# A decoder block's forward and backward on one core: the two layer norms and their gradients at the turn written as sums over shared means, with weights, dV groups and d(o) reordered

## The chip, the cores and the metric

One core of a Trainium2 chip runs the whole program. The metric is device time in microseconds (us), lower is better; the kernel before was timed in three runs. Engines: TensorE (PE, with its weight loads PEld), VectorE (DVE), ScalarE (ACT), GpSimd (POOL, here mostly a queue that issues stores) and SyncE (SP, the queue that issues loads).

## The reference: what is computed

One token goes forward through an adaptive-layer-norm block, attention over a cached K and V (32 heads, 8192 positions, 192 wide) and an MLP; then the gradients of the output with respect to x, K, V, wq, wo, w3, w4, c and w_mod are taken. Cut to what matters here:

```python
def _layernorm(x, axis=-1, eps=1e-05):
    m = jnp.mean(x, axis=axis, keepdims=True)
    v = jnp.var(x, axis=axis, keepdims=True)
    return (x - m) / jnp.sqrt(v + eps)
# _A_ref: q = x @ wq per head; p = softmax(q K^T * 192**-0.5); o = p V; returns o @ wo
# _B_ref, for one token (its mixer's shifted rows are all zero, so x1 = x):
    return x + _gelu(_layernorm(x) @ w3) @ w4
# the block:
mod = (_silu(c) @ w_mod)                      # sa, ca, ga, sb, cb, gb, 640 each
h = _layernorm(x) * (1 + ca) + sa
x = x + ga * _A_ref(h, k_cache, v_cache, wq, wo)     # x1 in the kernel
h = _layernorm(x) * (1 + cb) + sb                    # h_b in the kernel
x = x + gb * _B_ref(h, w1, w2, w3, w4)
# vjp with grad_out: outputs: x, and the gradients of the nine inputs named above; dK and dV are the largest
```

So between the last head's attention and the first gradient there are two layer norms one behind the other (of x1, then of h_b), the product with w3, a gelu, the products with w4 forward and backward, w3 backward, and the two layer norms' gradients. The gradient of the attention output, d(o) = (ga * dx1) @ wo^T, is what all dK and dV need.

## The kernel before

K and V of a head are 3 MB each and are streamed in halves of 1536 KB. Position p*64 + j of the cache lies on partition p, so a half is a tile of 128 x 32 x 192. There are five buffers for K (`KB`) and three for V (`VB`).

*Forward*, `for i in range(H1)`: per head the scores are a product on VectorE (`dot_mul`, L302), a halving add (L306) and a sum on TensorE against an identity (`dot_tree`, L312). One head later the softmax weights scale V (`scale_v`: some rows on VectorE, L352, the others one by one on ScalarE, L359), and TensorE multiplies the scaled V by K (`m_units`, L374 and L379: a 193-wide product that the gradient of q needs, in four quarters). `pair_ao` multiplies the outputs of two heads by wo. `wst` holds weights in flight: one buffer for tag `w`, two for tag `wo`.

*The turn* is everything from `x, y, z = X[H1], ...` (L568) to the first pass of the backward loop. Its order on PE, DVE, ACT and SP is as written (`manual_schedule(engines=ORDER)`): each engine and each queue runs its instructions in the order in which the code names them, and one that waits holds all behind it. In the turn the last head's (31) scores are taken in quarters into `pb`, head 30's scaled V tiles `vs0` to `vs3` are made and multiplied into `mp`, head 31's output goes through `o_rows` (L394), `pair_sums`, `pair_ao` to `aoN` (L709), and:

- `g_layernorm` (L141), twice: `x1` to `n1`, `h_b` to `n2`. Each takes a mean by a matmul with a matrix of 1/640 (`mean_mm`, L123) and a sum on VectorE (L128), centres, squares, takes a second mean, and the root as exp(-0.5 ln(.)) on ScalarE (L151, L152).
- `ups` (L767): 60 matmuls with w3; then the gelu (L773 to L792). `dg_part` (L476) is the dot of one w4 row group with `dbo_bc`, 12 in all on VectorE; `du_bf` (L795) needs them all.
- `w3t_gen` (L749, L750) transposes w3 in 12 groups of 5 blocks, ScalarE copying 640 columns each; `dn_ps` (L850) is the product with it.
- `layernorm_bwd` (L166), twice, then `dao_bf` (L918), `do_mm(TL, 1)` (L901): d(o) of head 31. Head 30 follows in the first round of the loop.
- `dw4_dve` (L802): outer products for dw4, in pieces where VectorE has room.
- w3 and w4 are loaded in nine transfers, two of them during head 29, into `w4b`, `wp`, a `wo` buffer, a `vs` buffer and K buffers that came free.

*Backward*, `for s in range(NS)`, 64 half heads from head 31 down: `mul_q` (L929) multiplies V by d(o), `tree_q` (L948) sums to dP (L316), dS follows (L1244), `dk_part` (L964) makes dK, `dv_groups` (L959, L960) makes dV in eight groups by TensorE and ScalarE copies; `dk_store` (L1214) and `dv_store` (L1210) are issued by POOL. A V half is loaded four half heads ahead, when the product that read the buffer is done. `c_ps` (L1223) sums dao * AO over columns for all heads: five fp32 matmuls with 32 columns. `side` jobs (dwq, dwo, dw_mod, dw3) are spread over the slots of the rounds.

## Time and profile before

| what | us |
|---|---|
| three runs | 1414.3, 1417.39, 1418.7 (median 1417.39) |
| the profiled execution's own time | 1418.06 |
| its span | 1416.1 |
| the turn by windows: DMA share at 531 to 549 | 0.98 |
| at 549 to 561 | 0.58 |
| at 561 to 573 | 0.26 |
| at 573 to 582 | 0.12 |
| at 582 to 600 | 0.74 |
| granted TensorE clock in the same five windows | 1.00, 0.86, 0.93, 0.50, 0.78 |

Busy shares of the span: TensorE 84%, VectorE 78%, ScalarE 63%. A busy share is an average over three stages with different limits (forward, turn, backward); the shares by window tell them apart. A timeline line reads: start in us, time of the merged group, engine, line of the code, operation, output tile <- input tiles, shapes, count, and in brackets the idle time in front of it and what ended it.

### The profile page before, as it was taken

The page shows a single profiled execution, that of the slowest core. Times are in us where ns is not written, and L with a number is a line of the kernel's source. Part 1 is how long each engine was busy: PE and PEld are TensorE (multiplying, and loading weights), DVE is VectorE, ACT ScalarE, POOL GpSimd, SP SyncE. Part 2 cuts the span into 40 slices and gives each one's busy share as a digit, 9 for nine tenths or more (in the row PEclk, how much of TensorE's full clock was granted, in tenths as well). Part 3 has the DMA queues.
Part 4 walks back from the last instruction along what each step waited for, and adds up shares of the span by engine and source line. Part 5 has one row for each costly group of instructions (what it writes and reads, how often), then busy time and mean ns, then how long its engine had stood idle before and what let it go on. Part 6 is the DMA issues. An engine that isn't in the chain of part 4 may idle for free.

```text
span 1416.1 us, 30395 instructions
## 1 busy us (share of the span) xinstructions
PE 1190.1 (84%) x12697; PEld 748.8 (53%) x12697; DVE 1108.4 (78%) x1418; ACT 893.9 (63%) x1952; POOL 105.3 (7%) x190
## 2 busy tenths in 40 slices
PE   3888989999999999798867997887978787779975
PEld 2777777777777777543323443443434333334431
DVE  4989999999999997886755875676766767768775
ACT  0767777777777776465645665565655565556664
POOL 0000000000000000110100110111110101111110
PEclk9999999999999999755555555565555655555555
DMA  9999999999999997599999999999999999999998
GB/s 375 394 394 416 418 415 418 411 415 414 422 415 419 411 412 274 178 391 428 424 393 420 427 423 424 420 422 422 425 420 421 411 414 410 405 400 392 424 411 355
DMA packets 76247, 569.35 MB, mean 402 GB/s; under 512 B 7342, under 2 KB 25086, under 8 KB 36046
## 3 DMA queue, kind: packets, MB, share of 16 engines
q1 hardware_dynamic: 51210, 342.02, 59.5%
q0 software_dynamic: 24368, 224.87, 38.1%
q8 instruction: 99, 1.62, 0.4%
q10 hardware_dynamic: 532, 0.53, 0.1%
q14 instruction: 38, 0.31, 0.1%
HBM read 340.95 MB, written 226.43 MB: 401 GB/s over the span
## 4 chain that ended last, share of the span: by engine, by line
issue 47%; DVE 22%; DMA 13%; PE 10%; POOL 6%; ACT 1%; SPq 0%; POOLq 0%; DVEq 0%
DVE prod L302 9%; DMA KB<-in_A_k_cache_dram 8%; DVE prod L306 5%; DVE vs L352 3%; PE mp L374 3%; DMA out_dram<-KB 3%; POOL out_dram L1214 2%; POOL out_dram L1210 2%; DMA w_st<-in_A_wq_dram 2%; PE half_ps L312 2%; PE mp L379 2%; DMA KB<-in_A_v_cache_dram 1%; DVE pq L929 1%; POOL out_dram L1054 1%; DVE KB L964 1%
## 5 line engine op out<-in xcount | busy, mean ns | idle before, releaser
L960 ACT CAST KB<-dv_ps 128x768 bf16<-128x768 f32 x512 | 397.4, 803 | 159.7 <-PE dv_ps L959 157.6
L948 PE MATMUL dot_ps<-pq,ident_bf 128*128 128x256 bf16 x1506 | 383.6, 398 | 24.0 <-DVE dP L316 22.0
L964 DVE TENSOR_TENSOR KB<-qs_bc,dS 128x3072 bf16<-128x3072 bf16 x122 | 210.7, 1753 | 129.0 <-DMA out_dram<-KB 117.0
L359 ACT ACTIVATE vs<-VB,Ef 128x192 bf16<-128x192 bf16 x840 | 303.5, 447 | 0.0
L948 PEld LDWEIGHTS <-ident_bf 128*128 128x128 bf16 x1506 | 151.9, 124 | 179.7 <-issue 140.3
L959 PE MATMUL dv_ps<-do_r,er_b 1*128 1x192 bf16 x2048 | 231.2, 338 | 4.5 <-ACT KB L960 3.2
L929 DVE TENSOR_TENSOR pq<-VB,do_r 128x3072 bf16<-128x3072 bf16 x126 | 220.4, 1749 | 15.7 <-PE dot_ps L948 15.7
L302 DVE TENSOR_TENSOR prod<-KB,qs_bc 128x6144 bf16<-128x6144 bf16 x62 | 207.9, 3353 | 26.6 <-DMA KB<-in_A_k_cache_dram 20.3
L374 PE MATMUL mp<-vs,KB 128*128 128x193 bf16 x1968 | 189.9, 249 | 3.7 <-ACT vs L359 2.6
L374 PEld LDWEIGHTS <-KB 128*128 128x128 bf16 x1984 | 171.1, 98 | 13.1 <-DMA KB<-in_A_k_cache_dram 5.3
L822 ACT COPY wT<-wT_ps 128x1024 bf16<-128x1024 bf16 x82 | 79.0, 964 | 122.6 <-PE wT_ps L821 122.2
L959 PEld LDWEIGHTS <-er_b 1*128 1x128 bf16 x2048 | 69.4, 104 | 157.5 <-issue 154.7
L312 PE MATMUL half_ps<-prod,ident_bf 128*128 128x256 bf16 x744 | 95.1, 279 | 44.4 <-DVE prod L306 44.1
L352 DVE TENSOR_TENSOR vs<-VB,E 128x1728 bf16<-128x1728 bf16 x120 | 123.7, 1052 | 0.3 <-ACT vs L359 0.3
L306 DVE TENSOR_TENSOR prod<-prod 128x3072 bf16<-128x3072 bf16 x62 | 108.7, 1754 | 1.0
L312 PEld LDWEIGHTS <-ident_bf 128*128 128x128 bf16 x744 | 72.9, 100 | 62.7 <-issue 53.6
L379 PE MATMUL mp<-vs,KB 128*64 128x193 bf16 x1968 | 105.9, 250 | 0.0
L316 DVE TENSOR_REDUCE dP<-dot_ps 128x32 f32<-128x512 f32 x64 | 44.0, 688 | 66.9 <-PE dot_ps L948 66.6
L379 PEld LDWEIGHTS <-KB 128*64 128x64 bf16 x1984 | 79.4, 109 | 20.0 <-issue 19.9
L339 ACT ACTIVATE E<-S_h,negm 128x256 bf16<-128x256 f32 x31 | 15.8, 508 | 113.9 <-DVE negm L502 111.6
L1214 POOL DMA_DIRECT2D out_dram<-KB x61 | 33.5, 549 | 475.5 <-DVE KB L964 299.8
L388 PE MATMUL op<-vs,ones_bf 128*32 128x193 bf16 x1920 | 62.1, 250 | 0.0
(300 smaller groups left out, 975.3 us busy)
## 6 DMA issues: line engine op xcount, KB each, us to landing
VB<-in_A_v_cache_dram SPq DMA_DIRECT2D x123, 1536.0 KB
out_dram<-KB POOLq DMA_DIRECT2D x123, 1536.0 KB, 16.0
KB<-in_A_k_cache_dram SPq DMA_DIRECT2D x64, 1536.0 KB
wo_st<-in_A_wo_dram SPq DMA_DIRECT2D x31, 480.0 KB
w_st<-in_A_wq_dram SPq DMA_DIRECT2D x12, 960.0 KB
out_dram<-wo_st POOLq DMA_DIRECT2D x16, 480.0 KB, 16.2
out_dram<-w_st POOLq DMA_DIRECT2D x7, 960.0 KB, 15.4
w_st<-in_w_mod_dram SPq DMA_DIRECT2D x6, 960.0 KB
```

Of the source, the lines that this page charges most:

```text
L302: V_.tensor_tensor(out=prod, in0=src, in1=vec[:, None, :].to_broadcast([P, JH, DH]), op=ALU.mult)
L306: V_.tensor_tensor(out=prod[:, :, 0:HW], in0=prod[:, :, 0:HW], in1=prod[:, :, DH - HW : DH], op=ALU.add)
L312: T_.matmul(ps, lhsT=ident_bf, rhs=prod[:, :, k : k + TF], start=(k == 0), stop=(k == w - TF))
L352: V_.tensor_tensor(out=vs[:, 0:n, 0:DH].rearrange("p j (a b) -> p j a b", b=4), in0=v[:, v0 : v0 + n, :].rearrange("p j (a b) -> p j a b", ...
L359: A_.activation(out=vs[:, k, 0:DH], in_=v[:, v0 + k, :], func=ACT.Copy, scale=Ef[:, j0 + k : j0 + k + 1])
L374: T_.matmul(mp[:, 0:MW], lhsT=kb[:, j0 + k, 0:P], rhs=vs[:, k, 0:MW], start=(q == 0 and k == 0), stop=(z and k == JQ - 1), skip_group_chec ...
L379: T_.matmul(mp[p0 : p0 + 64, MO : MO + MW], lhsT=kb[:, j0 + k, P:DH], rhs=vs[:, k, 0:MW], start=False, stop=(z and k >= JQ - 2), skip_grou ...
L929: V_.tensor_tensor(out=pq[:, q], in0=v_l[s][:, q * JQ : (q + 1) * JQ, :], in1=do_of(ht(s)[0])[:, None, :].to_broadcast([P, JQ, DH]), op=AL ...
L948: T_.matmul(ps[:, q * JQ : (q + 1) * JQ, :], lhsT=ident_bf, rhs=pq[:, q, :, k : k + TS], start=(k == 0), stop=(k == w - TS), skip_group_ch ...
L959: T_.matmul(ps[:, b, k * DH : (k + 1) * DH], lhsT=er[p0 : p0 + 1, 2 * m + k, :], rhs=doh[p0 : p0 + 1, :], start=True, stop=True)
L960: A_.copy(out=dV4[:, 2 * q : 2 * q + 2, m * PW : (m + 1) * PW], in_=ps[:, :, 0:PW])
L964: V_.tensor_tensor(out=dK[:, lo:hi, :].rearrange("p j (a b) -> p j a b", b=4), in0=qh.rearrange("p (a b) -> p a b", b=4)[:, None, :, :].to ...
```

## The change

Parts, in the order of the program:

1. `mean_cols`, `g_mean` and `g_layernorm` give way to plain `layernorm` (for x only); `mean_mm`'s PSUM tile grows from 16 to 32 columns.
2. `g_consts`, three steps at heads 24 and 25, computes what depends on the modulation alone: 1+cb, sb less its mean, their squares' and products' means, and `dbo`.
3. w3 row 4 and w4 row 0 are no longer loaded in head 29, wo's last rows not in head 30; behind the last V half come w4 rows 0 to 3 (into `w4b`), wo, then w3 rows 0 to 3 in one transfer into `wp`, w3 row 4 into a `wo` buffer, and w4 rows 4 to 7 and 8 to 11 into `KX`.
4. The scaled V tiles are shared differently: no VectorE part in `vs0` and `vs3`; `m_units` of quarters 1 to 3 stand at other places; pair 14's `pair_o` and `pair_ao` come earlier.
5. Six means in one matmul (`mo`: x, x*(1+cb), their squares, and two products with constants) give both norms' statistics; `rsqrt` is called twice with scalar steps between; x is centred by x's own first mean (`xc0`) before.
6. w3 is transposed in three thirds of 20 blocks, in groups of 8, 8 and 4, so ScalarE copies 1024, 1024 and 512 columns; four scalings of `vs3` stand between two of these.
7. The gradient of both norms is written as A*dn + B + NW*(four means), A, B, NW from a mean of five products (`sg`, `ps5`) taken before `dn` is there; `dao_bf` is computed by a version with ga multiplied in (`Ag`, `Bg`, `NWg`). dx1 and d_sb are computed after it (`dx1_out`, `d_sb_out`).
8. `do_mm` computes both heads of a pair in one group; the call in the first round is gone.
9. All four dV groups of the first half and its store stand ahead of the second tree; `c_ps` is one matmul after a product and a sum on VectorE.

```diff
-    def mean_cols(src, groups, name, fill=None):
...
+    def layernorm(x, name):
+        m = col(1, name + "_m")
+        V_.reduce_sum(out=m, in_=mean_mm(x, ND)[:, 0:ND], axis=AX.X)
...
+    def g_consts(res):
+        V_.tensor_scalar(out=cb1, in0=cb, scalar1=1.0, scalar2=None, op0=ALU.add)
+        ps = mean_mm(sb, ND)
+        yield
+        m = mean_sum(ps, 1, "sb_m")
+        V_.tensor_scalar(out=bt, in0=sb, scalar1=m[:, 0:1], scalar2=None, op0=ALU.subtract)
...
-                if i % 2 == 0 and i > 0:
+                if i % 2 == 0 and 0 < i < H1 - 1:
                     wo_l[i // 2] = load_wo(i // 2)
...
+                if i in (24, 25):
+                    next(cst, None)
...
-                if i == H1 - 2:
-                    nc.sync.dma_start(out=w4b[:, 0:F], in_=w3d[:, 4, :])
-                    nc.sync.dma_start(out=w4b[:, F : F + D], in_=w4v[:, 0, :])
...
             x["v"].append(load_v(H1, 1, KY))
+            load_rows(w4b[:, 0 : 4 * D], 0, 4)
+            wo_l[TL] = load_wo(TL)
...
+            nc.sync.dma_start(out=wp.rearrange("p (i n) -> p i n", i=4), in_=w3d[:, 0:4, :])
             dot_sum(d0, x["S"][:, 0:JH])
-            vs_dve(vs1, 1, JQ // 2, JQ)
+            o2 = pair_o(TL - 1, po)
             dot_sum(d1, x["S"][:, JH:J])
+            vs1 = new_vs(1)
+            vs_act(vs1, 1, JQ // 2, JQ - 2)
...
+            vs_dve(vs1, 1, 0, JQ // 2)
+            vs_act(vs1, 1, JQ - 2, JQ)
+            vs2 = new_vs(2)
+            vs_act(vs2, 2, JQ // 2, JQ // 2 + 3)
             vs_dve(vs2, 2, 0, JQ // 2)
+            pe.pop(0)()
             A_.copy(out=ox, in_=op_x[:, 0:DH])
+            vs_act(vs2, 2, JQ // 2 + 3, JQ)
...
+            pe = m_units(1, ky[0], vs1, mp)
+            pe.pop(0)()
+            pe.pop(0)()
+            aoN = col(ND, "aoN")
             V_.reduce_sum(out=aoN, in_=ps_ao, axis=AX.X)
+            V_.tensor_tensor(out=t0, in0=ga, in1=aoN, op=ALU.mult)
+            V_.tensor_tensor(out=mo[:, 0, :], in0=t0, in1=xP, op=ALU.add)
+            V_.tensor_tensor(out=mo[:, 1, :], in0=mo[:, 0, :], in1=cb1, op=ALU.mult)
+            V_.tensor_tensor(out=mo[:, 2:4, :], in0=mo[:, 0:2, :], in1=mo[:, 0:2, :], op=ALU.mult)
+            V_.tensor_tensor(out=mo[:, 4:6, :], in0=mo[:, 1:2, :].to_broadcast([P, 2, ND]), in1=cK, op=ALU.mult)
+            ps = mean_mm(mo.rearrange("p a b -> p (a b)"), 6 * ND)
             V_.tensor_copy(out=AO[:, :, 2 * TL : 2 * TL + 2], in_=ps_ao)
             dg_part(1)
...
+            S6 = mean_sum(ps, 6, "S6")
+            V_.tensor_scalar(out=nm, in0=S6[:, 0:1], scalar1=-1.0, scalar2=None, op0=ALU.mult)
+            V_.scalar_tensor_tensor(out=var, in0=S6[:, 0:1], scalar=nm, in1=S6[:, 2:3], op0=ALU.mult, op1=ALU.add)
+            rsqrt(r1, var)
...
+            V_.scalar_tensor_tensor(out=v1, in0=va, scalar=r1[:, 0:1], in1=cov, op0=ALU.mult, op1=ALU.add)
+            V_.scalar_tensor_tensor(out=var2, in0=v1, scalar=r1[:, 0:1], in1=k4[:, 3:4], op0=ALU.mult, op1=ALU.add)
+            rsqrt(r2, var2)
+            V_.tensor_scalar(out=ac, in0=ac, scalar1=nab, scalar2=None, op0=ALU.add)
+            V_.scalar_tensor_tensor(out=hx, in0=ac, scalar=r1[:, 0:1], in1=bt, op0=ALU.mult, op1=ALU.add)
             dg_part(1)
+            V_.tensor_scalar(out=n2_bf, in0=hx, scalar1=r2[:, 0:1], scalar2=None, op0=ALU.mult)
...
+            w3t()
+            pe = m_units(2, ky[1], vs2, mp)
+            pe.pop(0)()
+            pe.pop(0)()
             ups = psS.tile([P, NF], FP32, name="u_ps", tag="s")
...
             dg_part(2)
-            w3t(2)
+            w3t()
+            vs_act(vs3, 3, 12, JQ)
+            w3t()
...
+            V_.tensor_scalar(out=n2, in0=hx, scalar1=r2[:, 0:1], scalar2=None, op0=ALU.mult)
+            V_.tensor_scalar(out=n1, in0=mo[:, 0, :], scalar1=nm, scalar2=r1[:, 0:1], op0=ALU.add, op1=ALU.mult)
...
+            ps5 = mean_mm(sg.rearrange("p a b -> p (a b)"), 5 * ND)
             dg_part(NF)
             du_bf = col(NF, "du_bf", BF16)
...
+            do_t(TL, 0)
+            do_t(TL, 8)
+            sk = mean_sum(ps5, 5, "sk")
+            V_.scalar_tensor_tensor(out=NW[:, 0, :], in0=n1, scalar=sk[:, 0:1], in1=cb1c, op0=ALU.mult, op1=ALU.subtract)
...
+            V_.tensor_tensor(out=NWg, in0=NW, in1=ga[:, None, :].to_broadcast([P, 4, ND]), op=ALU.mult)
...
+            V_.scalar_tensor_tensor(out=B1, in0=vv, scalar=nr1, in1=dy_c, op0=ALU.mult, op1=ALU.add)
+            V_.tensor_tensor(out=Bg, in0=B1, in1=ga, op=ALU.mult)
...
+            dw4_dve(flat(KX), 0, 0, 3)
+            V_.tensor_tensor(out=pr, in0=dn_ps[:, None, :].to_broadcast([P, 4, ND]), in1=G, op=ALU.mult)
+            ps = mean_mm(pr.rearrange("p a b -> p (a b)"), 4 * ND)
+            V_.tensor_tensor(out=vg, in0=Ag, in1=dn_ps, op=ALU.mult)
+            V_.tensor_tensor(out=vg, in0=vg, in1=Bg, op=ALU.add)
+            s4 = mean_sum(ps, 4, "s4")
+            V_.tensor_tensor(out=q4, in0=NWg, in1=s4[:, :, None].to_broadcast([P, 4, ND]), op=ALU.mult)
+            V_.reduce_sum(out=qr, in_=q4.rearrange("p a b -> p b a"), axis=AX.X)
+            V_.tensor_tensor(out=dao_bf, in0=vg, in1=qr, op=ALU.add)
+            dw4_dve(flat(KX), 0, 3, 6)
...
-    layernorm_bwd(d_n2, n2, r2, dbo, d_sb, "lb2", ...)
-    layernorm_bwd(d_n1, n1, r1, dy_c, dx1, "lb1", ...)
-    do_mm(TL, 1)
-    dw4_dve(flat(KX), 0, 5, 9)
+    do_mm(TL, (1, 0))
+    V_.tensor_tensor(out=dao, in0=vg, in1=qr, op=ALU.add)
+    dx1_out()
+    d_sb_out()
+    dw4_dve(flat(KX), 0, 6, 9)
...
-    dv_groups(dV0, er, do_of(H1), (0, 2))
-    for k in range(ND):
-        T_.matmul(c_ps, lhsT=dao[:, k : k + 1].to_broadcast([P, P]), rhs=AO[:, k, :], start=(k == 0), stop=(k == ND - 1))
+    dv_groups(dV0, er, do_of(H1), (0, 2, 4, 6))
+    dv_store(0, dV0, 0, JQ)
...
+    V_.tensor_tensor(out=cx, in0=AO.rearrange("p k h -> p h k"), in1=dao[:, None, :].to_broadcast([P, HQ, ND]), op=ALU.mult)
+    V_.reduce_sum(out=cs, in_=cx, axis=AX.X)
+    T_.matmul(c_ps, lhsT=c32, rhs=cs, start=True, stop=True)
...
-        if s == 0:
-            do_mm(TL, 0)
```

## The prediction

> **What bounds the kernel now.** First the page's rows by slice, to see where the machine is full.
>
> ```profile
> DMA  9999999999999997599999999999999999999998
> GB/s 375 394 394 416 418 415 418 411 415 414 422 415 419 411 412 274 178 391 428 424 393 420 427 423 424 420 422 422 425 420 421 411 414 410 405 400 392 424 411 355
> ```
>
> The transfers are full from end to end, but for slices 16 and 17 (531 to 602 us). Then three stretches, by windows.
>
> ```profile
> 20.00:500.00 480.00, 428.67 (x6517) 359.33 (x6517) 444.98 (x420) 347.39 (x1131) 7.19 (x13) 0.99 1.01 412
> 544.00:600.00 56.00, 43.89 (x658) 36.07 (x656) 42.86 (x123) 26.73 (x60) 4.57 (x7) 0.80 0.52 174
> 604.00:1410.00 806.00, 666.27 (x4778) 312.28 (x4774) 569.87 (x810) 481.32 (x645) 91.92 (x161) 0.53 1.00 413
> ```
>
> Outside the turn the DMA share is 1.01 and 1.00: there the bytes set the time, and no engine does. In the turn it is 0.52 of 56 us, so 27 us of transfer time are lost. The bytes stay the same, so the change is worth what it takes off these 27 us, and nothing elsewhere. Which wait ends last in the turn, the chain says (start, us, what):
>
> ```profile
> 537.45 11.45 DMA KB<-in_A_v_cache_dram
> ...
> 562.48 1.48 PE u_ps L767 x60
> ...
> 574.76 1.59 PE dn_ps L850 x60
> ...
> 580.73 0.18 DVE dao_bf L918
> 580.96 0.99 PE do_ps L901 x5
> ...
> 583.27 2.27 PE c_ps L1223 x10
> ...
> 590.13 0.70 DVE dP L316
> ```
>
> It is one chain of small steps: the last V half lands (537.45 + 11.45 = 548.9), output of head 31, MLP forward, MLP backward, d(o), first scores of the backward. The stream starts again when the first V buffer of the backward comes free:
>
> ```profile
> 592.90 0.33 SPq L297 DMA_DIRECT2D VB<-in_A_v_cache_dram  x1
> ```
>
> That load waits for the product at 591.12, which follows dP at 590.13 through dS on VectorE without a gap. So I follow the chain to dP. What VectorE pays for small operations is in its timeline:
>
> ```profile
> 572.83 0.17 DVE L795 SCALAR_TENSOR_TENSOR du_bf<-t__10308,d_g 128x12 bf16<-128x12 f32 x1
> 572.92 0.17 DVE L796 SCALAR_TENSOR_TENSOR du<-t__10308,d_g 128x12 f32<-128x12 f32 x1
> 573.00 0.68 DVE L802 TENSOR_SCALAR KB<-w4b,g__10305 128x640 bf16<-128x640 bf16 x2
> ...
> 577.76 0.29 DVE L172 TENSOR_SCALAR lb_t<-ln_n,lb_s 128x5 f32<-128x5 f32 x1
> 578.09 0.17 DVE L174 TENSOR_TENSOR lb_t<-d_n,lb_t 128x5 f32<-128x5 f32 x1
> 578.29 0.23 DVE L175 SCALAR_TENSOR_TENSOR dmod<-lb_t,ln_r,dbo 128x5 f32<-128x5 f32 x1
> ```
>
> Independent ones start 0.08 to 0.09 us apart (572.83, 572.92, 573.00); one that needs the one before starts 0.20 later (578.09 to 578.29); with per-column scalars read from memory it lasts 0.23 to 0.29 and the next dependent one starts 0.27 to 0.33 later. Independent ones of that kind start 0.14 apart (n_bf 560.57, ln_n 560.71).
>
> **The change part by part,** as landmarks, before and after.
>
> *Loads.* w3 row 4 and w4 row 0 (544 KB) no longer stand in front of the last K half, nor those and the wo rows of pair 15 (1024 KB) in front of the last V half. At 413 GB/s that is 1.3 and 2.5 us. K: VectorE takes it at 540.19 after 0.31 idle; its own queue is free at 539.0 without vs_dve (0.95), so its product starts 1.1 earlier. V lands at 546.4. The moved bytes and the other loads follow on the same queue: w4 0-3, wo, w3 0-3 (2,656 KB, 6.6 us) are in by 553, needed at 555; w3 4 and w4 4-11 come after and hide behind the dots before them. Cover gone, each late microsecond would be one on the chain. *To head 31's output:* ScalarE has 16 + 6 scalings of 0.353 and three small ones ahead of the exponential and reaches it at 546.3 (547.20 before); V is there, 64 matmuls of 1.5 end at 548.3 (549.79). ScalarE's copy of it now stands behind five scalings: 549.1 against 549.84, so half the gain is lost. po 1.36, three steps 0.6, the wo product 0.65: aoN at 552.1 (553.52). Gain 1.4.
>
> *Norms.* Before: aoN to n_bf 7.3 us, with four means through TensorE (0.56 each, two matmuls) and two root pairs on ScalarE (0.55). After: five dependent steps 1.05; one mean of 30 columns, bounded by 0.57 (10 columns) and twice that, taken 0.62 since 5 and 10 columns differ by 0.01; it waits for 16 matmuls of quarter 1, queued in front of it (1.51), 0.4. S6, nm, var 0.6, root 0.55, v1 and var2 0.5, root 0.55, one dot (0.86) in VectorE's way, n2 0.25. Sum 5.4: 557.5 (560.80). Gain 3.3.
>
> That TensorE queue has a price that depends on the granted clock:
>
> ```profile
> 554.00:558.00 4.00, 3.76 (x28) 3.27 (x28) 3.11 (x13) 1.49 (x5) 0.00 (x0) 0.57 0.69 224
> 558.00:571.00 13.00, 11.88 (x256) 10.95 (x253) 9.95 (x36) 6.61 (x13) 0.54 (x1) 1.00 0.35 110
> ```
>
> At 0.57, 8 matmuls took 1.45 us (554.65), at 1.00 0.84 (545.15); 16 in front of the mean then cost 1.4 more. I take 1.00, as 549 to 571 holds no gap on TensorE above 1 us in my steps. The Trainium skill, "TensorE: Matmul & The Clock Gate", section "What's actually happening", has the array drop to half clock after an idle window of some 3.4 us; by it the sum stays at the full clock, and the trace agrees that the half clock here follows a thin stretch (TensorE busy 0.97 of 2 us at 552).
>
> *MLP.* u starts when n2 is there (557.65; before 562.31, TensorE late by 1.5) and ends at 559.2. But ScalarE's exponential is now behind a w3 copy of 1024 columns (1.0, as wT's), four scalings (1.4) and one of 512 (0.55): it ends 3.7 after u instead of 1.76, at 562.9 (565.69). Gain 2.8. Six small steps to t_ as before. Then eight new ones (n2, n1, rho, cn, copies, two products for five means) stand in front of the last dots: 0.9. Seven dots of 0.866 are left as before: du_bf at 571.0 (572.83). Gain 1.8.
>
> *Gradients.* Before: dn waits for w3 copies until 574.76, then 0.20 + 4.4 us of two layernorm_bwd to dao_bf (end 580.90). After: dn runs at 571.3 to 572.9, but VectorE first does 15 coefficient steps (1.95 at the pitches above), m_add 0.38, bo 0.08 and three dw4 rows of 0.3: the product with dn starts at 574.4. It, a mean (its matmuls behind two wT groups, which end at 574.85; 0.6), four steps: dao_bf ends at 576.3. Gain 4.6.
>
> *To the first d(o) product.* Both heads in one matmul group: 5 x 384 columns at 0.50 clock, 1.8 against 0.98; d(o) at 578.7 (582.4). VectorE meanwhile has six dw4 rows (2.0), dao, dx1 (0.9), d_sb, h_b, x1 (1.1): it arrives at 580.1. So VectorE decides: 582.43 becomes 580.1, gain 2.3; half of the 4.6 is given back to work that is only moved.
>
> *To dP.* Removed: ten c_ps matmuls (2.34 between 583.20 and 585.54); added: two VectorE steps 0.5 and one matmul pair, 0.6. VectorE: two products 3.45, 0.5, three dw4 0.97, cpr 0.2, one product 1.75: dP 6.9 after the first product (before 7.7), at 587.0, if the two trees (2.75 at half clock, 1.48 at full) are through; both at half end at 588.1. Gain 2.0 to 3.1, taken 2.6. All four dV groups and a store of 768 KB (1.9 us of transfer) move from 590.35 to 583, into empty time; on POOL's queue it now precedes the second dw4 store, whose rows are ready only at 585, so nothing waits for it. As the stretch 588 to 600 still has 3 us of holes, I count 0 to 1.0 of it, 0.4. The removed d(o) matmuls (0.59) and copy (0.44) of the first round lie beside VectorE's 592 to 598, worth 0. The constants computed at heads 24 and 25 (16 small steps, some 3 us, and two means) lie in DMA time: VectorE is busy 445 of 480 us there.
>
> Sum: 2.6 + 0.4 = 3.0. The profiled execution took 1418.06 (span 1416.1, 1.96 around it); 3.0 off is 1415.1. It lies 0.7 above the median of 1417.39, which gives 1414.4: my forecast.
>
> **Rivals.** *A, the whole gain arrives.* If VectorE's 35 filling steps between t_ and the first product (4.9 us above) start 0.08 apart, they take 2.8, d(o) comes earlier with them, and the first product starts at 578.0; with trees at full clock dP follows at 584.9: 5.2, and 0.4 of stores: 1411.8. For it: most of the filling is independent in pairs and trios, and VectorE idles 1.35 before the exponential in my steps, which gives room. Against: 22 of the 35 read a pointer scalar or the step before.
> *B, a new wait eats it.* Half clock over quarters 1 and 2 delays n2 by 1.4 and u by 1.5 more, and the dots then start as late as before: gain 0, 1417.4. For it: the clock did fall at 554. Against: VectorE has 1.35 idle to give, and c_ps is gone anyway.
> *C, slower: VectorE's small steps.* If each of the 35 holds the engine for 0.27 (a dependent pointer step) instead of my mean 0.14, it would be 4.6 more on the one engine that decides from 563 to 580: 2.0 slower, 1419.4; at 0.33 4.1 slower, 1421.5. It decides from a mean pitch of 0.21 up. Against it stands the 0.08 at 572.83. The Trainium skill speaks for it: "VectorE: DVE Perf Modes", section "The DRAIN you can't avoid", has the next operation wait until the pipe is empty; the row of 0.08 contradicts that for independent ones.
>
> **How the numbers follow.** Forecast (gain 1.5 to 4.2) 0.45, A 0.30, B 0.13, C 0.12. What a measurement here can tell from no change is about 0.3%, 4.25 us. A and a little of the forecast's upper end pass it: faster 0.34. C passes it only at its far end, with what I have not seen: slower 0.08. Same 0.58. The likeliest alone spans 1413.2 to 1415.9; the range must reach A's 1411.8 and its scatter, B, and C's 1419.4: 1410.5 to 1419.5.
>
> **What would show it.** Right: V landing near 546.4, aoN near 552, n2_bf near 557.5, an idle VectorE before the step after the exponential, dao_bf 4 to 5 earlier and the first d(o) product only 2 to 3 earlier with no idle in front of it. A: that product waits for ScalarE's d(o). B: clock under 0.7 between 552 and 560. C: mean pitch of the coefficient steps above 0.2. Wrong altogether: a DMA share under 0.97 after 604, or the turn's loss unchanged while its landmarks move.

## The result, and the profile after

The changed kernel takes 1409.15 us (median of 6 runs, 1408.45 to 1410.26); the kernel before took 1416.29 beside it (6 runs). The ratio is 0.9950, with a 95% interval of 0.9937 to 0.9963: 7.1 us less, where 3.0 were forecast and 1410.5 was the lower end of the range. Two more sittings (a sitting is a set of kernels timed together, the kernel before always among them) gave 0.9952 (0.9940 to 0.9964) and 0.9934 (0.9920 to 0.9948). The profiled execution took 1408.49 (span 1406.7). One execution of all, 2015.8 us in `loads_back`, was of the slow kind and is in no ratio below.

The same three windows as before, of the changed kernel (the third ends 10 us earlier; columns: stretch, its length, busy us and count of PE, PEld, DVE, ACT and POOL, granted clock, DMA share, GB/s):

```profile
20.00:500.00 480.00, 430.00 (x6568) 360.64 (x6568) 448.92 (x438) 347.58 (x1131) 7.15 (x13) 1.00 1.01 415
544.00:600.00 56.00, 45.14 (x644) 34.77 (x643) 47.34 (x150) 33.25 (x70) 4.53 (x7) 0.79 0.57 203
604.00:1400.00 796.00, 665.05 (x4735) 311.24 (x4727) 564.82 (x807) 476.88 (x639) 91.63 (x160) 0.52 1.00 415
```

The stream is as full as before outside the turn (1.01 and 1.00), so the limit has not moved. A full share does not fix the rate, though: at the same shares it was 412 and 413 GB/s before and is 415 and 415 here. In the turn the share went from 0.52 to 0.57: 2.8 of its 27 lost us are regained in this pair of profiles (later profiles have 0.48 before and 0.59 after).

The chain of waits of the changed kernel through the turn (start, us, what):

```profile
549.83 2.61 PE mp L402 x16
552.44 0.33 PE mean_ps L123 x2
...
556.13 1.65 PE u_ps L817 x60
...
569.52 1.74 PE dn_ps L904 x60
...
577.41 0.68 DVE KB L872 x2
...
584.77 0.64 DVE dP L344
```

`layernorm_bwd` and `c_ps` are gone from it. One mean is left in front of u, and it stands behind 16 matmuls that took 2.61 us here. The stream starts again 5.4 us earlier than before (592.90), on SyncE's queue:

```profile
587.48 0.34 SPq L325 DMA_DIRECT2D VB<-in_A_v_cache_dram  x1
```

VectorE's small steps, from its timeline:

```profile
569.30 0.17 DVE L859 SCALAR_TENSOR_TENSOR du_bf<-t__10323,d_g 128x12 bf16<-128x12 f32 x1
569.38 0.18 DVE L128 TENSOR_REDUCE sk<-mean_ps 128x5 f32<-128x25 f32 x1
569.60 0.23 DVE L911 SCALAR_TENSOR_TENSOR NW<-n,sk,cb1c 128x5 f32<-128x5 f32 x1
569.74 0.23 DVE L912 TENSOR_SCALAR w<-sg,sk 128x5 f32<-128x5 f32 x1
569.87 0.22 DVE L913 TENSOR_SCALAR w<-sg,sk 128x5 f32<-128x5 f32 x1
...
577.11 0.97 DVE L872 TENSOR_SCALAR KB<-w4b,g__10320 128x640 bf16<-128x640 bf16 x3
578.01 1.75 DVE L1028 TENSOR_TENSOR pq<-KB,do_r 128x3072 bf16<-128x3072 bf16 x1
```

Independent steps with a pointer scalar (one value per partition, read from memory) start 0.13 to 0.14 apart (569.60, 569.74, 569.87), a dependent one 0.22 after the sum. The first d(o) product starts straight behind the dw4 rows, with no idle time noted: VectorE decides there, as forecast.

**A measure that leaves the forward out.** Executions differ in when the turn begins, so I take all times in the turn from the first score product of head 31 (VectorE, `pb`). In us, with the start of each step:

| profile | first score product | to n2_bf | to u on VectorE | to dao_bf, end | to first d(o) product | to dP | dP to end of span |
|---|---|---|---|---|---|---|---|
| before | 533.53 | 27.0 | 30.5 | 47.4 | 48.9 | 56.6 | 826.0 |
| before_again | 533.06 | 27.9 | 32.4 | 49.4 | 50.9 | 58.4 | 823.5 |
| after | 530.73 | 25.1 | 27.4 | 43.7 | 47.3 | 54.0 | 822.0 |
| after_again | 531.12 | 24.0 | 26.2 | 42.5 | 46.1 | 52.9 | 824.7 |
| after_third | 531.84 | 23.9 | 26.2 | 42.5 | 46.1 | 52.9 | 824.4 |

My steps gave 54.0 for the way to dP in the changed kernel (587.5 less 533.53). The first profile has exactly that; the two others have 52.9. Before, it was 56.6 in the profile that I had and 58.4 in the next. The first pair thus shows a gain of 2.6, as forecast, but by luck: in both a half clock of 3.4 us fell in front of u (next section). The means (57.5 and 53.3) show 4.2. Three kernels of the experiments have the same turn as one of the two up to dP, or nearly: `before_part9` 56.6, `before_loads` 56.9, `loads_back` 52.9. With them the means are 57.1 and 53.2, a gain of about 4.

### The profile page after: what moved, and what is told of

The parts are those of the page before. It is cut to its first block, busy times and chain, and to the rows that moved or that the text cites. A ratio compares the mean times of both kernels' runs of the same rounds, so it can differ in the third digit from the quotient of the medians.

```text
span 1406.7 us, 30418 instructions
## 1 busy us (share of the span) xinstructions
PE 1191.4 (85%) x12687; PEld 747.4 (53%) x12687; DVE 1111.1 (79%) x1464; ACT 899.3 (64%) x1966; POOL 105.6 (8%) x190
## 4 chain that ended last, share of the span: by engine, by line
issue 44%; DVE 20%; DMA 16%; PE 12%; POOL 5%; ACT 2%; SPq 0%; POOLq 0%; DVEq 0%
DMA KB<-in_A_k_cache_dram 10%; DVE prod L330 8%; DVE prod L334 4%; DMA out_dram<-KB 4%; PE mp L402 3%; DVE vs L380 2%; PE half_ps L340 2%; POOL out_dram L1313 2%; POOL out_dram L1309 2%; DMA w_st<-in_A_wq_dram 2%; PE mp L407 2%; PE dot_ps L1047 1%; DVE pq L1028 1%; PE dv_ps L1058 1%; DVE KB L1063 1%
## 5 line engine op out<-in xcount | busy, mean ns | idle before, releaser
L1047 PE MATMUL dot_ps<-pq,ident_bf 128*128 128x256 bf16 x1506 | 386.5, 401 | 26.6 <-DVE dP L344 24.3
L340 PE MATMUL half_ps<-prod,ident_bf 128*128 128x256 bf16 x744 | 95.0, 279 | 44.6 <-DVE prod L334 44.1
```

Of the source, the lines that this page charges most:

```text
L340: T_.matmul(ps, lhsT=ident_bf, rhs=prod[:, :, k : k + TF], start=(k == 0), stop=(k == w - TF))
L1047: T_.matmul(ps[:, q * JQ : (q + 1) * JQ, :], lhsT=ident_bf, rhs=pq[:, q, :, k : k + TS], start=(k == 0), stop=(k == w - TS), skip_group_ch ...
```

## The experiments

Ratios are to the kernel before, in the same sitting, with 95% intervals; 0.001 is 1.4 us. The diffs are shortened, and a line in plain words stands for several of code. Places in the turn come from one profile of each kernel.

### Is it there again?

`after_again` and `after_third` are the changed kernel, `before_again` the one before.

> The changed kernel once more, unaltered, for a second profile of it and five more timed rounds. Theory 1, the surplus over my 3.0 is made by the change: 7 us below before again, the stretch behind dP again about 4 shorter than in the first profile of before. Theory 2, part of the surplus is scatter between executions: the gain comes nearer to 4 to 6 us, and the two places where the first pair of profiles differ in code that is the same (2.5 us in heads 4 to 8, 4 us behind dP) come out otherwise in this profile.

> The kernel before once more, for a second profile of it. Theory 1: span near 1416 and the heads 4 to 8 as late as in the first profile, since nothing there depends on the execution. Theory 2: heads 4 to 8 some 1 to 2.5 us earlier, and the stretch behind dP other than 826 us by 1 or more.

> The changed kernel a third time, as the measure for the three that run with it. If its gain is steady: 6.5 to 7.5 us below before, dP 52.9 us after the first score product, or 54 where the clock falls at 550. If 7 was luck of two sittings: 4 to 6.

Measured: 1410.39 us, 0.9952 (0.9940 to 0.9964), and 1408.77 us, 0.9934 (0.9920 to 0.9948); `before_again` took 1416.80. The gain is steady, so theory 1 holds for the total. Behind dP theory 2 holds: from dP to the end the spread within one kernel (822.0 to 824.7, and 823.5 to 826.0) is as large as the difference. In the early heads it is not shown here: the first product of head 8 starts at 152.7 and 152.5 in the two profiles of the kernel before, at 150.3, 151.2 and 150.0 in those of the changed one.

What does differ inside the turn is the granted clock. Windows of the changed kernel, first and second profile (columns as above):

```profile
550.00:553.00 3.00, 3.00 (x26) 2.79 (x25) 1.79 (x10) 2.20 (x7) 0.00 (x0) 0.56 0.87 296
```

```profile
550.00:553.00 3.00, 3.00 (x52) 2.75 (x48) 2.55 (x16) 2.90 (x9) 0.00 (x0) 1.00 0.87 265
```

The 16 matmuls in front of the mean, from TensorE's timeline, first and second profile:

```profile
549.70 2.75 PE L402 MATMUL mp<-vs,KB 128*128 128x193 bf16 x16
```

```profile
550.07 1.51 PE L402 MATMUL mp<-vs,KB 128*128 128x193 bf16 x16
```

They take 2.75 us at half clock and 1.51 at full: that is the 1.2 us by which n2_bf is later in the first profile. No idle stretch stands in front of this fall, which came at 549.2: TensorE is shown busy for 2.97 of the 3.41 us before it, with no gap above 0.29 (3.00 of 3.40 at the same place of the second profile, which did not fall). In `before_again` the half clock lasted from 552 to 562; up to 560.5 the window reads:

```profile
552.00:560.50 8.50, 7.70 (x66) 6.33 (x67) 6.55 (x29) 3.35 (x12) 0.00 (x0) 0.50 0.58 202
```

All four profiles of the kernel before and its variants without added products fall in front of u: for 3.4 us (`before`), 10.2 (`before_again`) and 6.8 (`before_loads`, `before_part9`). Of the 13 with the new norms three do (`after`, `dots_tail`, `warm`), each for 3.4.

### Part 9: the dV groups, the store and c

```diff
 # part9_undone: the changed kernel, first round as before
-    dv_groups(dV0, er, do_of(H1), (0, 2, 4, 6))
-    dv_store(0, dV0, 0, JQ)
+    dv_groups(dV0, er, do_of(H1), (0, 2))
+    for k in range(ND):
+        T_.matmul(c_ps, lhsT=dao[:, k : k + 1].to_broadcast([P, P]), rhs=AO[:, k, :], start=(k == 0), stop=(k == ND - 1))
     tree_q(ps, 0, 0)
     mul_q(0, 1)
-    cx, cs, c_ps = product, sum, one matmul
+    dv_groups(dV0, er, do_of(H1), (4, 6))
+    dv_store(0, dV0, 0, JQ)
 # before_part9: the kernel before with the opposite edit
```

> The changed kernel with the first round of the backward as before: dV groups in two pairs, the 768 KB store behind the second pair, c as five fp32 products on TensorE (scaled by rinv alone). If the moved store is worth the 0.4 that I counted and c_ps 0.4 to 0.8 of dP: 1 us slower than the changed kernel, 6 below before. If the early store is where the surplus comes from (768 KB are 1.9 us of transfer, taken out of the full stretch and put into the hole): 3 to 4 us slower than the changed kernel, 3 to 4 below before. dP would come 0.8 to 1.5 later after the first d(o) product.

> The kernel before with the changed first round of the backward alone: four dV groups and the 768 KB store ahead, c as a product, a sum and one matmul on VectorE and TensorE. By my steps (c 0.4 to 0.8 of dP, the store 0.4): 1 us below before. If the store in the hole is worth its whole 1.9 us of transfer: 2.5 to 3 below. If both are covered by other work: within 0.5. The first score product as in the run with the fillers.

Measured: undone 0.9963 (0.9949 to 0.9976), against 0.9952 for the changed kernel beside it; alone in the kernel before 0.9988 (0.9973 to 1.0003). Both are 1.6 to 1.7 us, and neither interval keeps out 0 to 3. From the first d(o) product to dP the undone kernel takes 8.0 us for 6.8, the kernel before with part 9 takes 7.5 where it took 7.5 and 7.7. So part 9 is worth 1.2 at dP in the changed kernel and about 0.1 in the kernel before; what it brought to the time there, if it did, is the store's. Where the 1.2 comes from, VectorE's timeline of the undone kernel shows:

```profile
586.11 0.69 DVE L344 TENSOR_REDUCE dP<-dot_ps 128x32 f32<-128x512 f32 x1 [1.64 <-PE dot_ps L1047]
```

There VectorE waits 1.64 for the second tree, with `c_ps` and both trees at half clock; in the changed kernel it has no wait in front of dP. My 0.3 at dP was too small by 0.9 in the changed kernel; whether my 0.4 for the store was, the time cannot tell.

### The loads

```diff
 # loads_back: the changed kernel, loads in front of the last K and V halves again
-                if i % 2 == 0 and 0 < i < H1 - 1:
+                if i % 2 == 0 and i > 0:
                     wo_l[i // 2] = load_wo(i // 2)
+                if i == H1 - 2:
+                    nc.sync.dma_start(out=w4b[:, 0 : 4 * D]..., in_=w4v[:, 0:4, :])
...
-            load_rows(w4b[:, 0 : 4 * D], 0, 4)
-            wo_l[TL] = load_wo(TL)
 # before_loads: the kernel before, its three loads behind load_v(H1, 1, KY)
```

> The changed kernel with loads in front of the last K and V halves again: four w4 rows (640 KB) ahead of the last K half, and the wo rows of the last pair at head 30 (480 KB), as many KB as before within a tenth. If the later loads bring the chain forward as I reckoned (half of 2.5 us lost behind ScalarE): the last V half 2.5 us later, head 31's output 1.2 to 2.5 later, the end 1.2 to 2.5 us above the changed kernel. If VectorE or ScalarE decide there: within 0.7 us of it.

> The kernel before with the order of loads alone changed: w3 row 4, w4 row 0 (544 KB) and the wo rows of the last pair (480 KB) go behind the last V half. Theory loads (the 1.3 us that the 544 KB took stood in front of all of head 31, not of its second K half alone, and came on top of my 1.4): from the first half head of head 28 to the first score product 58.9 us, as in five kernels with the late loads, against 60.0 in four with the early ones; aoN 2 to 2.5 us earlier than in before; the time 1.5 to 2.5 below before. As I predicted: 1.4 at aoN, about 1 below before. Rival (the loads only shift a wait, the earlier first product is scatter of the forward): 60.0 again, the time within 0.7.

Measured: 0.9965 (0.9951 to 0.9978) and 1.0001 (0.9989 to 1.0013). In `loads_back` aoN comes 19.12 us after the first score product, in the changed kernel 19.12: the second K half is used 1.1 later (6.7 for 5.5), and the wait is gone again by the exponential (13.74 both). In `before_loads` aoN comes at 19.3 instead of 20.0 and 20.3, and the time doesn't follow. The stretch of its expectation took 60.4 us, as with the early loads (60.0), not 58.9. That stretch begins, other than its text says, with the second product of head 27; from the first product of head 28 to the first score product it is 49.3 to 49.9 in all 20 profiles. So the 1.1 between 60.0 and 58.9 lies in head 27, behind the new constants (see "Constants at nothing" below), and has nothing to do with these loads.

By the traces the rival holds: the late loads shift a wait. The time of `loads_back`, 1.8 above the changed kernel beside it, lies in the range of the first theory, but its interval (some 2.5 to either side) reaches 0, and dP is where it was (52.9).

### Norms, and the clock

```diff
 # before_fill: the kernel before
+            fill = psR.tile([P, 512], FP32, name="fill_ps", tag="dot_ps")
+            for _ in range(4):
+                T_.matmul(fill, lhsT=ident_bf, rhs=flat(ky[1])[:, 0:512], start=True, stop=True)
             ps_ao = pair_ao(o2, wo_l[TL], psB, "b")
 # norm_undone: the changed kernel, four means of 5 columns in place of one of 30
-            ps = mean_mm(mo, 6 * ND); moments, rsqrt(r1, var), v1, var2, rsqrt(r2, var2)
+            mean of x1, xc1, sq, mean of sq, rsqrt(r1, .), ac = xc1 * r1 * cb1 + sb,
+            mean of ac, hx, sq, mean of sq, rsqrt(r2, .), n2_bf = hx * r2
 # norm_fill: the same with 4 and 3 such idle products behind the second and third mean
```

> The kernel before with four idle products of 128x128 by 128x512 on TensorE, into a bank that nothing reads, where it waits 0.99 us for o of head 31 in front of the last wo product; nothing else is changed. Theory clock (the half clock that follows that gap, 4 us long in the first profile and 10 in the second, is a cost of the chain before, which my steps left at what the first profile showed): the granted clock stays at 1.00 from 550 to 568, n2_bf comes 1 us (against the first profile) to 2 us (against the second) earlier after the first score product of head 31 (27.0 and 27.9), and the time falls by 1 to 2.5 us. Rival (the clock falls for another reason, or the chain does not wait for TensorE): the same clock, and within 0.7 us of before or slower by the 1 us that the fillers take. The first score product itself, near 533.3 in two profiles of before and 530.6 to 532.0 in four that have the change: near 533 again if the 2 us in front of the turn belong to the kernel before, anywhere from 531 to 533.5 if they are scatter.

> The changed kernel with two layer norms one behind the other on the way to n2 (four means of 5 columns, each norm's variance from centred values), in place of the six moments at once; the rest, constants too, stays. The way from aoN to n2_bf took 7.05 and 7.65 us in before and 4.8 in three of four profiles of the changed kernel (5.98 with half clock): n2_bf 2.0 to 2.8 later after the first score product, and dP and the end 2 to 2.8 us above the changed kernel if nothing else waits. Rival (ScalarE's queue in front of the exponential hides part): 1 or less above it.

> The kernel with the norms undone (norm_undone), and in it seven idle products of 128x128 by 128x512 on TensorE in its two waits between the means (1.24 and 0.81 us). Theory clock (most of the norms' worth is that TensorE stays at full clock): clock 1.00 from 552 to 566, the 16 matmuls in front of u 1.5 for 2.8, u 27.5 to 28.5 after the first score product (30.7 without the fillers, 26.2 in the changed kernel), dP 54.5 to 55.5, the time 2 to 3.5 us below norm_undone, 2 to 3 above the changed kernel. Rival (the chain's length is the cost): u at 30 or later, the time within 1 of norm_undone.

Measured: `before_fill` 0.9999 (0.9984 to 1.0015), `norm_undone` 0.9997 (0.9983 to 1.0011), `norm_fill` 0.9970 (0.9955 to 0.9984). The windows of the three, in this order:

```profile
552.00:562.00 10.00, 8.24 (x112) 6.40 (x113) 8.53 (x34) 4.14 (x14) 0.00 (x0) 1.00 0.76 243
```

```profile
555.00:565.00 10.00, 9.19 (x121) 8.47 (x122) 5.22 (x19) 4.75 (x12) 0.00 (x0) 0.50 0.19 64
```

```profile
555.00:565.00 10.00, 8.92 (x152) 7.46 (x151) 6.28 (x25) 6.53 (x16) 0.00 (x0) 1.00 0.23 67
```

With four idle products in a gap of 0.99 us the clock stays at 1.00 in the kernel before: n2_bf comes at 26.6 (27.0 and 27.9 without), dP at 56.3 (56.6 and 58.4). The time shows none of it: its interval reaches from 2.3 us below to 2.1 above, so the 1 us and more of the expectation can't be told from nothing.

With the norms undone the whole gain is gone (0.9997). n2_bf comes at 26.2, 2.25 later than in the changed kernel, as expected. Then comes what I had not expected: the 16 matmuls of quarter 2 in front of u and u itself run at half clock, u is there at 30.7 (26.2), and dP at 58.3 (52.9). So of the 5.4 us, 2.25 are the chain's own length, 2.2 are added between n2_bf and u, and 0.9 behind it. `norm_fill` brings the second part back: with the clock at 1.00 it is 2.5 us from n2_bf to u instead of 4.5, and the time is 3.8 us below that of `norm_undone` (another sitting; the intervals just touch). Its own n2_bf is at 27.3, because the clock in this execution was 0.50 from 550 to 553, ahead of the fillers, where the first 16 matmuls took 2.75. So u is there at 29.9 and dP at 57.0, later than the clock theory's 27.5 to 28.5 and 54.5 to 55.5, and the time is 5.1 above the changed kernel beside it, for 2 to 3 expected. Both theories hold a part: the clock's share is about the 2.0 us that the fillers took off between n2_bf and u, the chain's length is 2.25.

### The gradient as a map

```diff
 # grad_undone: the changed kernel
-            rho, cn, sg, ps5 and the 15 coefficient steps; pr with G, s4, q4, qr
+            lb(d_n2, n2, r2, dbo, d_sb, ...)
+            d_n1 = cb1 * d_sb
+            lb(d_n1, n1, r1, dy_c, dx1, ...)
+            dao_bf = dx1 * ga
-    dx1_out()
-    d_sb_out()
```

> The changed kernel with two layer norm gradients one behind the other, as before (two means of 10 columns), in place of the map of four means; the eight steps and the mean of 25 columns behind n2 and the 15 coefficient steps fall away, and dx1 and d_sb are there without the moved steps. The other parts stay. By my steps the map gains 2.8 up to dao_bf and gives back 0.9 in front of the last dots and about 1.3 behind dao_bf, so that it is worth 0.6 at the first d(o) product: this kernel 0 to 1 us above the changed one, dao_bf 2 later, the first d(o) product 0.5 later. Rival (the map is a large part of the 7): 2.5 to 3 us above it.

Measured: 0.9977 (0.9961 to 0.9992), 3.5 us or more above the changed kernel. The turn shows what I expected: dao_bf 1.7 later (44.2), the first d(o) product 0.4 later (46.5), dP 1.0 later (53.9). Behind dP its profile has 829.0 us to the end, the longest of all, but that execution took 1418.3, the second slowest of 12 and 4.4 above their median, so the place of the other 2.5 is not known. By its steps the map is worth 1 us; the time says more, and I have no wait that accounts for it.

### VectorE in front of the first d(o) product

```diff
 # tail_light: dx1_out() and d_sb_out() behind the load that the first dS releases
 # dots_ahead: the changed kernel
             V_.tensor_tensor(out=e1, in0=e1, in1=u, op=ALU.mult)
-            dg_part(1)
+            dg_part(3)
 # dots_tail: dots_ahead, and dx1_out() and d_sb_out() in g_small, one slot more
 # warm: dots_ahead, and two idle products behind dn, two behind the mean of pr
```

> The changed kernel with dx1, d_sb, h_b and x1 (11 small steps of VectorE) put behind the V load that the first dS releases; the dw4 rows and their store stay ahead, so that their bytes stay in the hole. If VectorE decides when the first d(o) product starts (578.0 and 577.2, no idle before it, while d(o) of the first head is there 1.3 earlier): that product 1.3 earlier after dao_bf, dP 0.8 to 1.3 earlier (the sum over the first tree may then decide), the end 0.8 to 1.3 us below the changed kernel. If TensorE's sums at half clock decide dP anyway: dP and the end within 0.4.

> The changed kernel with two of the seven last dots of d_g put into the 1.6 us in which VectorE waits for ScalarE's exponential; nothing is added or left out. If VectorE's queue sets du_bf (as I took it): du_bf 1.5 to 1.7 earlier after the first score product of head 31, dn, dao_bf and dP with it, the end 1.5 us below the changed kernel. If w4 rows 5 and 6 are not there yet, or the w3 copies on ScalarE set dn: less than 0.5.

> The kernel with two dots in the exponential's wait once more, beside the changed kernel. If the 1.3 us at dP is 1.3 us of the time: 1 to 1.5 below the changed kernel of this sitting. If the end does not follow the turn: within 0.5 of it or above.

> The changed kernel with the two dots in the exponential's wait (1.3 of dP when tried alone) and the 11 small steps of dx1, d_sb, h_b and x1 taken to the later rounds of the backward where their results are first used, instead of behind the first dS, where they made the second round 1.9 us longer (9.5 for 7.66) and the time 3 us worse. If VectorE decides until the stream is full again, and not behind that: first d(o) product 44.8 - 1.5 = 43.3 after the first score product, dP 50.9 to 51.3, the second round at 7.66, the end 0.5 to 1 below the kernel with the dots alone, 1.5 to 2.5 below the changed kernel. If the later rounds are as sensitive to VectorE's work: no better than with the dots alone.

> The kernel with two dots in the exponential's wait, and on TensorE four idle products of 128x128 by 128x512, two behind dn's narrow products and two behind the mean of the gradient, to keep the clock up from 570 to 583, where every profile has it at 0.50. If that holds it: the d(o) products 0.9 for 1.8, the first sum 1.5 for 2.7, dP 49.5 to 50.5 after the first score product (51.6 and 51.8 without the fillers), the end 1 to 2 us below the changed kernel. If the clock falls all the same: dP 52 or later and the time that of the kernel with the dots or up to 1 above it.

| kernel | ratio (interval) | first d(o) product | dP | dP to end |
|---|---|---|---|---|
| tail_light | 0.9975 (0.9958 to 0.9991) | 44.8 | 52.2 | 827.5 |
| dots_ahead | 0.9947 (0.9931 to 0.9963) | 44.6 | 51.6 | 823.7 |
| dots_again | 0.9950 (0.9936 to 0.9965) | 44.4 | 51.8 | 822.2 |
| dots_tail | 0.9985 (0.9967 to 1.0003) | 44.0 | 51.4 | 827.3 |
| warm | 0.9951 (0.9932 to 0.9970) | 45.6 | 53.0 | 825.1 |

With the small steps gone the first product starts 1.3 earlier, which confirms that they held it. But both kernels that move them end 3 us or more behind the changed one. In `tail_light` the place shows, in VectorE's timeline:

```profile
583.81 0.35 DVE L1343 SCALAR_TENSOR_TENSOR dS<-dP,cpr,E_all 128x128 bf16<-128x128 f32 x1
584.08 1.75 DVE L1026 TENSOR_TENSOR pq<-VB,do_r 128x3072 bf16<-128x3072 bf16 x1
585.75 0.17 DVE L947 TENSOR_TENSOR pr<-NW,s 128x20 f32<-128x20 f32 x1
...
587.60 3.42 DVE L1061 TENSOR_TENSOR KB<-qs_bc,dS 128x3072 bf16<-128x3072 bf16 x2
...
593.32 0.35 DVE L1343 SCALAR_TENSOR_TENSOR dS<-dP,cpr,E_all 128x128 bf16<-128x128 f32 x1
```

The second dS comes 9.5 us after the first, where all others have 7.66: this round runs at VectorE's pace, and the 1.85 us of small steps put into it are paid in full there. That this is why the time is worse is not shown: in `dots_tail` that round is 7.66, and the time is no better; this I can't explain.

The two dots bring 1.3 and 1.1 at dP. In the time they are not to be told from the changed kernel (0.9947 and 0.9950 against 0.9934 to 0.9952; 0.9950 against 0.9934 side by side), so no kernel tried here is shown to beat it. In `warm` the clock fell all the same, as the second half of its expectation has it: the idle products, two and two, raise it to 0.68 and 0.74 between 572 and 580, and at 580 it is 0.50 again, for both trees (it had also fallen in front of u, which makes 1.1 of the 53.0):

```profile
572.00:576.00 4.00, 3.43 (x20) 1.52 (x18) 3.32 (x21) 2.15 (x5) 0.00 (x0) 0.68 0.03 6
576.00:580.00 4.00, 1.74 (x15) 1.07 (x13) 3.96 (x9) 2.83 (x4) 1.59 (x2) 0.74 0.22 78
580.00:584.00 4.00, 4.00 (x21) 2.91 (x20) 3.94 (x10) 0.00 (x0) 0.77 (x1) 0.50 1.01 364
```

### Is a microsecond of the turn one of the time?

```diff
 # delay2; delay4 has range(4)
+    for _ in range(2):
+        dw4_dve(flat(KX), 0, 3, 6)
     dx1_out()
     d_sb_out()
```

> The changed kernel with three dw4 rows computed three times instead of once, 1.8 us more on VectorE between dao_bf and the first d(o) product; the output is the same. If a microsecond of the turn is a microsecond of the time: first d(o) product 47.9 and dP 54.7 after the first score product, the end 1.8 above the changed kernel. If the time of the backward depends on something else (where the refilled stream happens to start against the stores): the end anywhere from 0 to 5 above, with a wider scatter.

> The changed kernel with three dw4 rows computed five times, 3.6 us more on VectorE in front of the first d(o) product; the output is the same. dP then comes 56.5 to 57 us after the first score product, as in before (56.3 to 58.4). If the time follows the turn 1:1: 3.6 us above the changed kernel, 3 to 4 below before, and then half of the 7 us are not in the turn. If the turn is all: within 1 us of before. With 1.8 us the time rose by 3 to 5.

Measured: dP at 55.0 and 56.4 (52.9 without), the times 0.9967 (0.9956 to 0.9979) and 0.9981 (0.9967 to 0.9995). With 2.1 us more in the turn the gain goes from 9.4 (0.9934, same sitting) to 4.7 us; with 3.5 more 2.7 are left, where the three sittings of the changed kernel have 6.8 to 9.4. A slope of 1 lies within the intervals, for `delay2` at their edge, and the slope is rather above it: 2.2 in `delay2`, 1.2 to 1.9 in `delay4`. And with a turn of 56.4 the changed kernel is still 2.7 us faster (0.7 to 4.7) than the kernel before, whose two profiles have 56.6 and 58.4. Less the 1.1 to their mean, 1.6 is left outside the turn, with an interval that reaches 0. So the first of its two theories is the likelier one, but that the turn is not all is not shown.

## Why the prediction was wrong

The direction, the order of the steps and what decides at each were right. Two terms of the sum were too small: the turn's 2.6 and the 0.4 outside it.

**The turn, 2.6: measured 4.2.** My steps for the changed kernel were good: from aoN to u 7.1 (measured 7.1), u to the exponential's end 3.7 (3.2), then to du_bf 8.1 (8.0), to dao_bf 5.3 (5.1), to the first d(o) product 3.8 (3.6). To dP I had 6.9 to 8.0, by the clock of the trees, and took the middle; it was 6.8. In all, 54.0 forecast and 53.3 measured, 0.7 of the missing 1.6. The other 0.9 is the other side of the subtraction, and there the step failed. I took the way of the kernel before from one execution, at 56.6; the second has 58.4, because the half clock that I read at 554 to 558 lasted 10 us there. I had named the clock's price for the changed kernel and put its fall among the rivals; that the old chain pays it too, every time another amount, I left out. "I take 1.00, as 549 to 571 holds no gap on TensorE above 1 us" came true in two of the three profiles of the changed kernel, but its reason failed: the other one fell with no gap above 0.29 in the 3.41 us in front. And "Norms ... Gain 3.3" (1.9 without the loads' 1.4) and "MLP ... Gain 2.8" counted the chain's length alone: undone, the norms cost 2.25 at n2_bf and 4.5 at u.

**Outside, 0.4: measured about 2.9,** that is 7.1 less 4.2; by `delay4` it would be 1.6. Either figure is good to some 2 us. What failed is the sentence "the change is worth what it takes off these 27 us, and nothing elsewhere", with 0.4 for the moved store, as far as the 2.9 are real. The spans of the two profiles before and the three after show where it lies: their means differ by 7.4, of which 2.1 are there at the first score product, 4.2 come in the turn and 1.1 behind dP. The cause is open; there are three candidates:

- *Part 9* is the one piece whose worth outside was tried: 1.6 in time less 1.2 at dP where it was undone, 1.7 less 0.1 where it stood alone, so 0.4 to 1.6, with intervals that reach 0.
- *The stretch in front of the turn.* The first score product is 1.1 earlier on average (531.6 in 15 profiles with the changed forward, 532.7 in 5 with the old one), but the ranges, 530.1 to 533.6 and 531.5 to 533.6, lie in one another. The difference is there at head 8 already (150.9 for 151.7), where both kernels issue the same loads and products. Over that stretch the stream's rate is 411 to 415 GB/s from one profile to the next, at a share of 1.01 in all. Whether the executions or the change made it stays open.
- *A slope above 1.* If a microsecond of the turn is worth more than one of the time, as `delay2`, `delay4` and `norm_undone` (5.4 at dP, 6.4 to 9.0 in time) hint, part of the 2.9 is the turn's. Against it, the 1.3 of the two dots did not show in the time.

**Point by point.**
- *Loads* (1.4 at aoN): wrong. aoN came 0.9 to 1.2 earlier after the first score product, but equally so with the loads in front; 0.8 of it comes from the shorter way from rinv to aoN (1.2 for 2.0). In absolute time V was used at 545.5, near the 546.4 of my steps, but only because this turn began 2.8 earlier: after the first score product it is 14.8, where my steps had 12.9 and the kernel before 15.4.
- *Constants at nothing:* nearly right, with the cover that I named. VectorE is 1.6 later behind them, and in the second half of head 27 it waits less. VectorE's timeline there, before:

```profile
481.82 0.42 DVE L316 TENSOR_REDUCE S_h<-half_ps 128x32 f32<-128x256 f32 x1 [1.01 <-PE half_ps L312]
...
484.25 3.36 DVE L302 TENSOR_TENSOR prod<-KB,qs_bc 128x6144 bf16<-128x6144 bf16 x1 [1.75 <-DMA KB<-in_A_k_cache_dram]
```

And after:

```profile
481.46 3.36 DVE L330 TENSOR_TENSOR prod<-KB,qs_bc 128x6144 bf16<-128x6144 bf16 x1 [1.61 <-DMA KB<-in_A_k_cache_dram]
```

Before, it idled 2.8 us in this half head, after, 1.6; in both a K half ends it. The lead, by how much the changed kernel is earlier, had gone down from 3.14 at head 24 to 1.54 and is back at 2.79 at head 28, so 0.35 of the 1.6 stayed. In all profiles heads 24 to 27 take 66.2 us on average with the constants and 65.7 without.
- *Gradients* (4.6 earlier, half given back): right in its parts, 8.1 from du_bf to dao_bf before, 5.1 after, and 2.1 of 3 given back in front of the first product.
- *First d(o) product:* VectorE decides, shown by the row at 578.01 and by `tail_light`.
- *Rival A* (whole gain, 1411.8) came nearest in time but not by its mechanism: the first product did not wait for d(o).
- *Rival B* (half clock eats it): the fall came in one of three profiles of this kernel, and cost 1.2. The 1.5 more at u did not come.
- *Rival C* (steps of 0.27): pitch 0.13 to 0.14 in the coefficient steps. Out. The section of the Trainium skill that this rival names, "The DRAIN you can't avoid" in "VectorE: DVE Perf Modes", also says that a next operation that is not held starts earlier; so the row of 0.08 need not contradict it, as I had written.

The Trainium skill, "TensorE: Matmul & The Clock Gate", section "What's actually happening", says that the activity window runs freely, so that the place of the change of clock differs between runs of one kernel. The profiles agree: the same code fell in one of three. So a single profile was no measure of this stretch.

## What to carry to other kernels

Here a serial stretch with thin work on TensorE paid twice: for its own length (2.25 us of the norms) and for the half clock of the matmuls behind it (2.0 to 2.2). Before you subtract from a profile, ask which of its durations depend on the granted clock, and take two profiles, or bound the old side as carefully as the new one. Work that is moved behind the restart of a stream is not free: in `tail_light` 1.85 us of it made a round 1.85 us longer.

## What the runs showed of the hardware that I had not expected

- In all 20 profiles the clock falls to 0.50 behind h2 (60 products of one column), from 0.2 us before its end to 2.7 us behind it. In the six with the old gradient that is 3.7 to 5.5 us ahead of the end of dn, in the others 1.9 us ahead of it to 1.2 us behind. TensorE is shown busy for 6.1 of the 9 us ahead of the fall in `after_third`; what the clock counts as work is not shown. Ahead of the fall and behind it:

```profile
561.00:570.00 9.00, 6.10 (x140) 5.53 (x140) 8.35 (x34) 5.81 (x12) 1.07 (x2) 1.00 0.22 64
571.50:583.00 11.50, 8.77 (x52) 5.65 (x51) 10.74 (x41) 5.46 (x8) 1.59 (x2) 0.50 0.28 98
```

- The half clock in front of u lasted 3.4, 6.8 or 10.2 us wherever it came (nine profiles), never anything between.
- With four products of 512 columns in a gap of 0.99 us the clock stayed up for the 10 us behind it (`before_fill`, one profile, where all four without them fell); with two and two in a thinner stretch it did not (`warm`).
- From dP to the end, at a DMA share of 1.00, the profiles differ between 822 and 829 us, three of the changed kernel alone by 2.7; most of the changes tried here are worth less.
